# Linear attention and a bilinear GLU on one core: an order found offline, uneven row blocks, denominators on four partition groups, GpSimd out of layernorm, Wq turned by DMA

## The chip, the cores and the metric

The kernel runs on one core of one Trainium2 chip. The core has a matrix engine (TensorE, PE in the profile, with PEld for its weight loads), a vector engine (VectorE, DVE), an activation engine (ScalarE, ACT), a general engine (GpSimd, POOL) and an engine that here only issues transfers (SyncE, SP). Each runs its own program in order and waits on semaphores for the others. The metric is the device time of one execution in microseconds; smaller is better.

## What is computed

Two sublayers on x of 2048 rows by 640 columns, all inputs bf16: layernorm and linear attention of 32 heads of 20 columns with a learned feature map (a softmax of +pq and one of -pq, side by side), then layernorm and a gated unit without a nonlinearity.

```python
def A(x, wqkv, w_phi, wo):                       # 32 heads, Dh = 20
    q, k, v = heads(x @ wqkv)
    pq, pk = q @ w_phi, k @ w_phi                # per head, 20 x 20
    phi_q = concat(softmax(pq), softmax(-pq))    # 40 features
    phi_k = concat(softmax(pk), softmax(-pk))
    kv, z = phi_k.T @ v, sum_over_rows(phi_k)    # per head
    o = (phi_q @ kv) / (phi_q @ z + 1e-6)
    return o @ wo
def B(x, w_gate, w_up, w_down):                  # F = 1536
    return ((x @ w_gate) * (x @ w_up)) @ w_down
h = x + A(layernorm(x), ...)
out = h + B(layernorm(h), ...)
```

## The kernel before

**Tiles and stages.** Rows come in 16 tiles of 128. Attention cannot start on queries until kv and z are summed over all rows, so the kernel has a first part over all tiles and a second one in blocks.

The *first part*, tile by tile: load x, statistics of layernorm (`ln_stats`, L669 and L671 on DVE; `ln_rs`, L591 on ACT and L677 on DVE), the row apply (`ln_apply`: L682 if on ACT, L685 if on DVE, L687 if on POOL), a transposing DMA into `xnT` (L574, on SP). Then the V projection and the K projection, ten matmuls each (`proj`, recorded by `mm` at L580), two exponentials of K on ACT (L591), and `normalise`: a row sum (L721) and a reciprocal (L723) on DVE into a buffer of `sr`, of which there are four, and a multiplication by it on POOL (L597, `r<-r,sr`). `kv_acc` then adds the tile to three PSUM accumulators with eleven matmuls over groups of six heads. The feature weights `w_phi` are folded into Wk and Wq ahead: `fold_T` turns a weight chunk on PE (25 transposes at L698 and five copies at L608 or L609 per weight), `fold_M` multiplies it with a block-diagonal `Phi` (30 matmuls) and `copy` brings the result back to SBUF (L609, `wq<-ps`). Wk is folded at the start, Wq after tile 3.

The *second part* has four blocks of four tiles (512 rows). `q_proj` projects Q, takes four exponentials on ACT, a row sum (L757), a reciprocal (L759) and a multiplication on POOL (L597, `phq<-phq,sr`), and turns the tile by DMA into `pqT`. `num` computes, for six groups of heads, numerators and denominators in one matmul: `KV` (filled by `kv_evac`, L597 and L826) holds z in its first six columns, so the first six PSUM rows of a product are denominators. ACT takes Ln and Exp of these six rows by 512 columns (L591, `lnd` and `rden`), PE spreads the result over the heads' rows with the 0/1 matrix `Em`, ACT (L875) or DVE (L876) copies that out, and DVE multiplies (L597). `watt` applies Wo and adds the residual (L888), centres the row (L892 on ACT, L893 on DVE, L894 on POOL), turns it by DMA into `hT`, and squares it in place for the variance (L896). `fu` computes gate and up for one of 12 column chunks (ten matmuls of 512 columns), `fd` applies w_down and the residual (L926) and stores.

**What sets the order.** The functions do not issue instructions; they record them with their reads, writes, buffers and an estimated cost (`Recorder.add`, `R.group` for PE's groups). Where an operation could run on several engines, `alts` lists the others. `schedule` builds the dependence graph, replays the list on the estimated costs in `simulate` several times with changing priorities, and keeps the order and the choice of engines of the shortest replay. `resolve` then finds the waits, and `emit` writes every engine's program in that fixed order. Buffers of a pool, and PSUM banks, are handed out in that replay too: an instruction that needs a buffer waits on the chip for the one that used it last. Transfers stand on SP's queue in the same fixed order.

The profile shortens buffer names: `r` stands for `r1` (Wk and Wq work space, `phik`, later `w_down` and the GLU's products) and `r2` (V, later the attention's output, gate copies and output tiles).

Of the kernel before, what the change touches and what calls it, by code (L numbers as in the profile page):

```python
# [134 lines left out]
class Recorder:  # L135
# [125 lines left out]
    def simulate(self, key, back=False):  # L261
# [28 lines left out]
        def try_start(e):  # L290
            skipped, got = [], None
            while ready[e]:
# [11 lines left out]
                for b in sorted(u.bufs, key=lambda b: b.n):  # L304
# [59 lines left out]
    def schedule(self):  # L364
        self.graph()
        units = self.units
        best = None
# [9 lines left out]
        best = self.simulate(best_key)  # L377
# [108 lines left out]

def bass_sequential_preLN__linear_kernel_hedgehog__glu_gated_bilinear__prompt_kernel(
# [5 lines left out]
def _build(ctx, nc, A_x, A_wqkv, A_w_phi, A_wo, B_w_gate, B_w_up, B_w_down, out):  # L493
# [10 lines left out]
    hT = xnT_r[:, :].rearrange("p (b c n) -> p b c n", b=NB, c=NC)  # L504
# [30 lines left out]
    pqT_p = Pool("pqT", [sb("pqT", NCH * 512)[:, :], wkv_r[:, 0:NCH * 512]])  # L535
    xn_p = pool("xn", sb("xn", 3 * D), 0, D, 3)
    KV = view(sb("KV", NCH * P), "p (c n) -> p c n", c=NCH)
# [11 lines left out]
    Em = sb("Em", P)  # L549
# [20 lines left out]
    def dma(dst, src, nbytes, reads=None, writes=None, tr=False, eng="sync"):  # L570
        rd = [src] if reads is None else reads
        wr = [dst] if writes is None else writes
        if tr:
            return R.add("sync", lambda e: e.dma_start_transpose(real(dst), real(src)), rd, wr,  # L574
                         cost=0.4 + 0.55 * nbytes / 163840, lat=1.3, dma=1.25 * nbytes / 163840)
        return R.add(eng, lambda e: e.dma_start(real(dst), real(src)), rd, wr, cost=0.5, lat=1.5, dma=nbytes / 350e3)

    def mm(o, l, r, start, stop, skip=False):
        kw = {"skip_group_check": True} if skip else {}
        return R.add("tensor", lambda e: e.matmul(real(o), lhsT=real(l), rhs=real(r), start=start, stop=stop, **kw),  # L580
                     [l, r], [o], cost=max(0.06, numel(r) / 2400.0 + 0.0025), lat=0.17)

    def act(o, i, func, scale=1.0, bias=None):
# [8 lines left out]
        return R.add("scalar", go, rd, [o], cost=0.17 + n / 1200.0, lat=0.08)  # L592

    def tt(eng, o, a, b, op):
        n = numel(o)
        cost = 0.18 + 0.0017 * n if eng == "gpsimd" else (n + 130) / 960.0
# [54 lines left out]
    memset("gpsimd", vaug[:, :, :].rearrange("p t (h e) -> p t h e", e=E21)[:, :, :, DH:E21], 1.0)  # L651
    phq_clear = memset("gpsimd", phq_r[:, :].rearrange("p (k n) -> p k n", n=P)[:, :, 80:P], 1.0)
    memset("gpsimd", KV[:, 10, 0:HG], 0.0)
    memset("gpsimd", G6[:, :], 1.0)
    memset("gpsimd", Em[:, :], 1.0)
# [7 lines left out]
    afsel(Em[:, :], ALU.is_ge, 0.0, -HG, [[1, P]], -DH)  # L663
    afsel(Em[:, :], ALU.is_ge, 0.0, HG + DH - 1, [[-1, P]], DH)
# [15 lines left out]
    def ln_apply(t, dst):  # L680
# [3 lines left out]
              [x_all[:, t, :], mv[:, t, 0:5]], [k], cost=0.86, lat=0.08,  # L684
              alts=[("vector", lambda e: e.tensor_scalar(out=real(k), in0=x_all[:, t, :], scalar1=mv[:, t, 0:1],  # L685
                                                         scalar2=mv[:, t, 3:4], op0=ALU.subtract, op1=ALU.mult), 0.7),
                    ("gpsimd", lambda e: e.tensor_scalar(out=real(k), in0=x_all[:, t, :], scalar1=mv[:, t, 0:1],  # L687
                                                         scalar2=mv[:, t, 3:4], op0=ALU.subtract, op1=ALU.mult), 1.1)])
# [3 lines left out]
    def fold_T(w, a):  # L692
        pb = psum.new(1)
        tb = pb.bitcast(BF16)
        with R.group():
            for a2 in range(NC):
                o, i = tb[:, P * a2:P * (a2 + 1)], Wnat[w][:, a2, P * a:P * (a + 1)]
                R.add("tensor", lambda e, o=o, i=i: e.transpose(out=real(o), in_=i, identity=ident[:, :]),  # L698
                      [i, ident[:, :]], [o], cost=0.08, lat=0.17)
        copy("any", WT[w][:, a, :], tb[:, 0:D])  # L700

    def fold_M(w, i, dst):
        pr = psum.new(2)
        first = [True, True]
        with R.group():
            for a in range(NC):
                lo, hi = CH[a]
                for (h0, h1, half) in [(lo, min(hi, 24), 0), (max(lo, 25), hi, 1)]:
                    if h0 > h1:
# [4 lines left out]
                       first[half], False, skip=True)  # L714
# [102 lines left out]
    def kv_evac(c, n):  # L817
# [7 lines left out]
        o, i = KV[0:kr, c:c + n, 0:nh], psv[:, :, :, DH]  # L825
# [4 lines left out]
    pqT = {}  # L830
    num_u = {}

    def q_proj(t):
        b, tt_ = divmod(t, 4)
        if b not in pqT:
            pqT[b] = pqT_p.new()
        pr = psum.new(2)
        with R.group(hold=[pqT[b]]) as u:
            proj(pr, t, Wq)
        if b >= 1:  # L840
            R.after(mark["kv_proj"], u)
            R.after(mark["q0"], u)
        elif t == 0:
            mark["q0"] = u
            R.after(phq_clear, u)
        if b >= 2:
            R.after(num_u[b - 2], u)
        k = phq_p.new()
        soft_q(pr[:, 0:D], k)
        dma(pqT[b].rearrange("p (c n) -> p c n", c=NCH)[:, :, P * tt_:P * (tt_ + 1)], k, NCH * 32768, tr=True)  # L850
# [4 lines left out]
    def num(b, c):  # L855
        if c == 0:
            oT[b] = oT_p.new()
        h0, nh, kr = chunk_heads(c if c < NG else 10)
        m = HG + DH * nh
        pr = psum.new(2)  # L860
# [182 lines left out]
```

## Time and profile before

| | |
|---|---|
| time, median of 3 runs | 331.82 us (331.55 to 333.7) |
| the profiled execution | 334.79 us, of which the span from its first to its last instruction is 333.1 us |
| mean granted TensorE clock | 0.964 |
| busy over the span | PE 302.5 us (91%), DVE 171.7 (52%), ACT 158.1 (47%), POOL 117.1 (35%) |
| DMA | 55466 packets, 25.82 MB; HBM read 11.87 MB, written 2.62 MB |

All times in a profile are in us from the span's start unless marked ns. A timeline row has start, length, engine, line, operation, output<-input, count; in brackets the engine's idle time before it and what ended that wait. A row of the groups has engine, line, operation, shapes and count, then busy time and mean ns of one, then idle time before them. A mean clock below 1.00 in a stage means that the matrix engine ran part of it at half speed.

### The profile page before, as it was taken

How to read it: one execution, taken by the hardware profiler on the slowest of the kernel's cores; microseconds unless marked ns; L12 is line 12 of the kernel's file. 1: busy time of each engine (PE TensorE's matmuls, PEld its weight loads, DVE VectorE, ACT ScalarE, POOL GpSimd, SP SyncE). 2: the span in 40 equal slices, each digit the busy share in tenths (PEclk: the TensorE clock that was granted, in tenths of full speed). 3: DMA queues.
4: the chain of work that ended last, by engine and by line, in shares of the span. 5: the costliest groups of instructions: out<-in, count | busy, mean ns of one | idle time of the engine just before them, and what ended most of it. 6: DMA issues, size and time to landing. Idle time of an engine off the chain costs nothing.

```text
span 333.1 us, 4763 instructions
## 1 busy us (share of the span) xinstructions
PE 302.5 (91%) x1890; PEld 156.2 (47%) x1890; DVE 171.7 (52%) x288; ACT 158.1 (47%) x333; POOL 117.1 (35%) x74
## 2 busy tenths in 40 slices
PE   2899759699977888999999999999999999999996
PEld 2656525355652333544445434445544445544453
DVE  3896455786666388756332265623245542233332
ACT  4886547476627556847221373542065264022200
POOL 8899777799586044755000000500000000000000
PEclk9999899799977599999999999999999999999999
DMA  7667025486947205645202100321100030100011
GB/s 245 171 146 213 10 50 159 122 206 218 229 127 161 45 5 100 108 90 99 45 0 59 41 0 0 61 44 41 52 8 0 2 68 14 59 0 2 0 39 61
DMA packets 55466, 25.82 MB, mean 78 GB/s; under 512 B 45935, under 2 KB 54163, under 8 KB 55443
## 3 DMA queue, kind: packets, MB, share of 16 engines
q1 hardware_dynamic: 53299, 22.89, 28.5%
q10 hardware_dynamic: 2144, 2.62, 2.5%
q8 instruction: 15, 0.25, 0.3%
q14 instruction: 8, 0.07, 0.1%
HBM read 11.87 MB, written 2.62 MB: 44 GB/s over the span
## 4 chain that ended last, share of the span: by engine, by line
PE 69%; POOL 16%; DVE 8%; issue 3%; ACT 2%; DMA 2%; DVEq 0%
PE ps L580 68%; POOL r L597 7%; POOL xn L687 5%; POOL phq L597 4%; DVE sr L721 3%; DMA r<-in_A_wqkv_dram 2%; DVE sr L757 1%; DVE r L597 1%; DVE x_all L888 1%; PE ps L698 1%; DVE r L876 1%; POOL xn L894 1%; ACT r L591 0%; ACT r L609 0%; DVE xn L893 0%
## 5 line engine op out<-in xcount | busy, mean ns | idle before, releaser
L580 PE MATMUL ps<-xnT,wgu 128*128 128x512 bf16 x480 | 106.6, 379 | 0.4 <-DVE r L597 0.2
L591 ACT ACTIVATE r<-ps 128x640 bf16<-128x640 f32 (+1 forms) x96 | 60.3, 648 | 76.3 <-PE ps L580 75.4
L597 DVE TENSOR_TENSOR r<-ps,r 128x512 bf16<-128x512 f32 (+2 forms) x72 | 48.2, 686 | 54.1 <-PE ps L580 47.5
L580 PE MATMUL ps<-r 128*128 128x512 bf16 (+5 forms) x620 | 71.2, 274 | 5.4 <-POOL r L597 2.7
L580 PEld LDWEIGHTS ps<-xnT,wgu 128*128 128x128 bf16 x480 | 45.9, 98 | 57.3 <-issue 1.8
L580 PEld LDWEIGHTS ps<-r 128*128 128x128 bf16 (+2 forms) x620 | 45.8, 111 | 30.8 <-POOL r L597 3.1
L580 PE MATMUL ps<-wkv,xnT 128*128 128x512 bf16 x320 | 48.7, 311 | 8.0 <-ACT wq L609 3.8
L597 POOL TENSOR_TENSOR phq<-phq,sr 128x1320 bf16<-128x1320 bf16 x16 | 38.6, 2424 | 24.6 <-DVE sr L759 16.9
L580 PEld LDWEIGHTS ps<-wkv,xnT 128*128 128x128 bf16 x320 | 25.4, 101 | 28.5 <-ACT wq L609 4.2
L597 POOL TENSOR_TENSOR r<-r,sr 128x1280 bf16<-128x1280 bf16 x16 | 37.3, 2356 | 3.7 <-DVE sr L721 3.7
L721 DVE TENSOR_REDUCE sr<-r 128x64 f32<-128x1280 bf16 x16 | 23.6, 1477 | 21.6 <-POOL r L597 15.7
L926 DVE SCALAR_TENSOR_TENSOR r<-ps,mv,x_all 128x640 bf16<-128x640 f32 x16 | 14.1, 883 | 36.0 <-PE ps L580 36.0
L591 ACT ACTIVATE phq<-ps 128x600 bf16<-128x600 f32 (+1 forms) x64 | 23.7, 443 | 15.8 <-PE ps L580 15.7
L580 PE MATMUL ps<-wo,r 126*128 126x512 bf16 x192 | 30.0, 300 | 0.7 <-DVE x_all L888 0.6
L580 PE MATMUL ps<-wq,xnT 128*128 128x512 bf16 (+1 forms) x160 | 28.4, 335 | 1.1 <-DVE r L597 1.1
L894 POOL TENSOR_SCALAR xn<-x_all,mv 128x640 bf16<-128x640 bf16 x4 | 7.5, 1883 | 60.4 <-DVE mv L602 58.6
L757 DVE TENSOR_REDUCE sr<-phq 128x66 f32<-128x1320 bf16 x16 | 24.2, 1520 | 8.2 <-POOL phq L597 4.0
L687 POOL TENSOR_SCALAR xn<-x_all,mv 128x640 bf16<-128x640 bf16 x10 | 24.9, 2498 | 8.6 <-DVE mv L677 8.6
L580 PEld LDWEIGHTS ps<-wo,r 126*128 126x128 bf16 x192 | 13.9, 97 | 16.3 <-issue 5.5
L580 PEld LDWEIGHTS ps<-wq,xnT 128*128 128x128 bf16 x160 | 13.7, 108 | 14.4 <-issue 5.5
L876 DVE CAST r<-ps 126x512 bf16<-126x512 f32 (+1 forms) x14 | 9.5, 687 | 19.4 <-PE ps L580 19.4
L591 ACT ACTIVATE lnd<-ps 6x512 f32<-6x512 f32 (+1 forms) x24 | 13.4, 580 | 12.6 <-PE ps L580 12.6
(56 smaller groups left out, 184.1 us busy)
## 6 DMA issues: line engine op xcount, KB each, us to landing
out_dram<-r SPq DMA_DIRECT2D x16, 160.0 KB, 1.8
x_all<-in_A_x_dram ACTq DMA_DIRECT2D x3, 640.0 KB, 4.6
wgu<-in_B_w_gate_dram SPq DMA_DIRECT2D x5, 384.0 KB, 4.7
wgu<-in_B_w_up_dram SPq DMA_DIRECT2D x5, 384.0 KB, 4.0
r<-in_B_w_down_dram SPq DMA_DIRECT2D x6, 320.0 KB, 4.6
r<-in_A_wqkv_dram SPq DMA_DIRECT2D x2, 800.0 KB, 5.1
wkv<-in_A_wqkv_dram SPq DMA_DIRECT2D x1, 800.0 KB, 10.0
wo<-in_A_wo_dram SPq DMA_DIRECT2D x4, 157.5 KB
```

Source lines behind the costliest of these rows:

```text
L580: return R.add("tensor", lambda e: e.matmul(real(o), lhsT=real(l), rhs=real(r), start=start, stop=stop, **kw), [l, r], [o], cost=max(0.06, ...
L591: return e.activation(out=real(o), in_=real(i), func=func, scale=scale, **kw)
L597: return R.add(eng, lambda e: e.tensor_tensor(out=real(o), in0=real(a), in1=real(b), op=op), [a, b], [o], cost=cost)
L687: ("gpsimd", lambda e: e.tensor_scalar(out=real(k), in0=x_all[:, t, :], scalar1=mv[:, t, 0:1], scalar2=mv[:, t, 3:4], op0=ALU.subtract, op ...
L698: R.add("tensor", lambda e, o=o, i=i: e.transpose(out=real(o), in_=i, identity=ident[:, :]), [i, ident[:, :]], [o], cost=0.08, lat=0.17)
L721: R.add("vector", lambda e: e.tensor_reduce(out=real(sr)[:, 0:n], in_=real(v), axis=AX.X, op=ALU.add), [v], [sr[:, 0:n]], cost=0.13 + n * ...
L757: R.add("vector", lambda e: e.tensor_reduce(out=real(r4(0)), in_=real(k4), axis=AX.X, op=ALU.add), [k4], [r4(0)], cost=0.13 + n * DH / 960.0)
L876: alts=[("vector", lambda e: e.tensor_copy(real(o), real(i)), 0.67)])
L888: R.add("vector", lambda e: e.scalar_tensor_tensor(out=h, in0=real(pr)[:, 0:D], scalar=1.0, in1=h, op0=ALU.mult, op1=ALU.add, accum_out=sm ...
L894: ("gpsimd", lambda e: e.tensor_scalar(out=real(k), in0=h, scalar1=nm, scalar2=None, op0=ALU.add), 1.1)])
L926: R.add("vector", lambda e: e.scalar_tensor_tensor(out=real(k), in0=real(pr)[:, 0:D], scalar=r2, in1=h, op0=ALU.mult, op1=ALU.add), [pr[:, ...
```

## The change

Six things are changed together.

1. **The order** is no longer searched while the program is built: a table `ORDER` of 1088 priorities, found offline, is replayed once. Some cost estimates are changed with it, and buffers are taken in the order of pool names. Every engine's program is reordered by this.
2. **Row blocks** are 2, 2, 4, 4 and 4 tiles (`BLK`) in place of 4, 4, 4 and 4. The first two blocks' numerators, gate and up matmuls have 256 columns. `q_proj` of the first two tiles no longer waits for all K and V projections by an explicit edge, and the edges between blocks are gone.
3. **Denominators of the first two blocks** (`num_first`): z is kept in a matrix `Zd` of 32 columns per group of heads. Up to four groups write their denominators to rows 0, 32, 64 and 96 of one PSUM bank, so that one Ln and one Exp over 128 rows by 256 columns serve four groups, and a second pair over 64 rows the other two. `Em` becomes four matrices, one for each starting row. The other blocks do it as before, with z copied from `Zd` into `KV`.
4. **GpSimd** has no row applies any more, neither in the first layernorm nor in the second; two memsets go from it to DVE, and memsets of the larger `Em` and of `Zd` come to it.
5. **Wq** is turned by five transposing DMAs straight out of DRAM, in place of one plain load, 25 transposes on PE and five copies.
6. **The square** of the second layernorm reads the row itself with the mean as bias and writes to `junk`, where it squared the centred row in place after its DMA.

```diff
-        best = self.simulate(best_key)
+        if len(ORDER) == len(units):
+            return {u: float(k) for u, k in zip(units, ORDER)}
...
+        best = self.simulate(self.keys())
...
+ORDER = [int(k) for k in """
+6 0 16 7 1 11 12 24 2 17 19 13 30 43 49 39 45 51 5 8 3 14 27 10 4 15 18 9 29 32 21 25 22 34 37 42 56 58 61 66 69 73 47 52 36 40 44 48 38 46 50 53 20
...
-    hT = xnT_r[:, :].rearrange("p (b c n) -> p b c n", b=NB, c=NC)
+    BLK = ((0, 2), (2, 2), (4, 4), (8, 4), (12, 4))
+    hT = [xnT_r[:, t * D:(t + n) * D].rearrange("p (c n) -> p c n", c=NC) for t, n in BLK]
...
-    memset("gpsimd", vaug[:, :, :].rearrange("p t (h e) -> p t h e", e=E21)[:, :, :, DH:E21], 1.0)
-    phq_clear = memset("gpsimd", phq_r[:, :].rearrange("p (k n) -> p k n", n=P)[:, :, 80:P], 1.0)
+    memset("vector", vaug[:, :, :].rearrange("p t (h e) -> p t h e", e=E21)[:, :, :, DH:E21], 1.0)
+    phq_clear = [memset("vector", phq_r[:, :].rearrange("p (c n) -> p c n", n=P)[:, :, 120:P], 1.0),
...
+    memset("gpsimd", Zd[:, :, :], 1.0)
...
               alts=[("vector", lambda e: e.tensor_scalar(out=real(k), in0=x_all[:, t, :], scalar1=mv[:, t, 0:1],
-                                                         scalar2=mv[:, t, 3:4], op0=ALU.subtract, op1=ALU.mult), 0.7),
-                    ("gpsimd", lambda e: e.tensor_scalar(out=real(k), in0=x_all[:, t, :], scalar1=mv[:, t, 0:1],
-                                                         scalar2=mv[:, t, 3:4], op0=ALU.subtract, op1=ALU.mult), 1.1)])
+                                                         scalar2=mv[:, t, 3:4], op0=ALU.subtract, op1=ALU.mult), 0.7)])
...
-        o, i = KV[0:kr, c:c + n, 0:nh], psv[:, :, :, DH]
+        o, i = Zd[0:kr, c:c + n, 0:nh], psv[:, :, :, DH]
...
+    def num_first(b):
+        oT[b] = oT_p.new()
+        q, n = pqT[b], P * BLK[b][1]
+        den = psum.new(1)
+        lnd, rden = lnd_p.new(), rden_p.new()
+        for k, cs in enumerate(((0, 1, 2, 3), (4, 5))):
+            bank = den[:, n * k:n * (k + 1)]
+            with R.group() as u:
+                for s in range(2):
+                    for j, c in enumerate(cs):
+                        kr = 120 if c < NG else 80
+                        ck = (NG * s + c) if c < NG else 10
+                        if c < NG or s == 0:
+                            mm(bank[32 * j:32 * j + 32, :], Zd[0:kr, ck, :], q[0:kr, ck, :], s == 0, s == 1 or c == NG,
+                               cost=0.06 if j else 0.25)
+            R.after(mark["kv_acc"], u)
+            w = 32 * len(cs)
+            act(lnd[0:w, n * k:n * (k + 1)], bank[0:w, :], ACT.Ln)
+            act(rden[0:w, n * k:n * (k + 1)], lnd[0:w, n * k:n * (k + 1)], ACT.Exp, scale=-1.0)
+        for c in range(6):
+            pr = psum.new(2)
+            nh, m, n = num_mm(b, c, pr)
+            r0, k = 32 * (c % 4), c // 4
+            expand(b, c, pr, m, Em[r0:r0 + nh, c % 4, 0:m], rden[r0:r0 + nh, n * k:n * (k + 1)])
...
-        R.add("scalar", lambda e: e.activation(out=real(k), in_=real(k), func=ACT.Square, accum_out=ss), [k], [k, ss],
-              cost=0.9, lat=0.08)
+        R.add("scalar", lambda e: e.activation(out=junk[:, :], in_=h, func=ACT.Square, bias=nm, accum_out=ss), [h, nm],
+              [junk[:, :], ss], cost=0.95, lat=0.08)
...
-            R.after(tr_u[5], load_w(Wnat[1], 0))
-            for a in range(NC):
-                fold_T(1, a)
+            for k in range(NC):
+                u = dma(WT[1][:, :, P * k:P * (k + 1)], A_wqkv[P * k:P * (k + 1), 0:D], 163840, reads=[], tr=True)
+                R.after(tr_u[5], u)
...
+    copy("any", KV[:, :, 0:HG], Zd[:, :, 0:HG])
```

Three places of the new order follow. A row of the order has line, operation, output<-input, the output's shape and how often it stands there in a row; the line numbers of the changed kernel are its own.

POOL in the first part, before: row applies (`xn`) stand between the normalisations of K (`r<-r,sr`).

```order
L687 TENSOR_SCALAR xn<-x_all,mv 128x640 x5
L597 TENSOR_TENSOR r<-r,sr 128x1280 x5
L687 TENSOR_SCALAR xn<-x_all,mv 128x640 x2
L597 TENSOR_TENSOR r<-r,sr 128x1280
L687 TENSOR_SCALAR xn<-x_all,mv 128x640
L597 TENSOR_TENSOR r<-r,sr 128x1280
```

POOL there now, from the making of `Phi` on to the end of its program:

```order
L645 TENSOR_TENSOR r<-Wrows,Gm 128x160
L645 TENSOR_TENSOR r<-Wrows,Gm 128x140 x4
L645 TENSOR_TENSOR r<-r,sr 128x1280 x8
L645 TENSOR_TENSOR phq<-phq,sr 128x11x120
L645 TENSOR_TENSOR r<-r,sr 128x1280 x3
L645 TENSOR_TENSOR phq<-phq,sr 128x11x120
L645 TENSOR_TENSOR r<-r,sr 128x1280 x5
L645 TENSOR_TENSOR phq<-phq,sr 128x11x120 x14
```

The ten row applies are gone, and two tiles of Q, where it was four, are normalised ahead of the last of K.

SP's queue from its start, before: the third row of `in_A_wqkv_dram` is Wq's plain load, behind seven turns of x tiles.

```order
L576 DMA r<-in_A_wqkv_dram 128x5x640
L576 DMA Wrows<-in_A_w_phi_dram 128x5x20
L576 DMA wkv<-in_A_wqkv_dram 128x5x640
L574 DMA_TRANSPOSE xnT<-xn 128x5x128 x7
L576 DMA r<-in_A_wqkv_dram 128x5x640
L574 DMA_TRANSPOSE xnT<-xn 128x5x128 x5
```

SP's queue from its start now:

```order
L624 DMA r<-in_A_wqkv_dram 128x5x640
L624 DMA Wrows<-in_A_w_phi_dram 128x5x20
L624 DMA wkv<-in_A_wqkv_dram 128x5x640
L622 DMA_TRANSPOSE xnT<-xn 128x5x128 x6
L622 DMA_TRANSPOSE r<-in_A_wqkv_dram 128x5x128
L622 DMA_TRANSPOSE xnT<-xn 128x5x128 x2
L622 DMA_TRANSPOSE r<-in_A_wqkv_dram 128x5x128 x4
```

Five transposing DMAs out of DRAM stand where the load stood, the first behind six turns of x tiles, the other four behind eight; the rows of `Wo` and of the gate and up weights come after them, and the ninth turn of x behind those.

ACT behind the last accumulation, before: Ln and Exp of six rows for each group of heads (`lnd`, `rden`), and the copies of the expanded denominators (L875).

```order
L591 ACTIVATE lnd<-ps 6x512 x2
L591 ACTIVATE rden<-lnd 6x512 x2
L591 ACTIVATE lnd<-ps 6x512
L875 ACTIVATE r<-ps 126x512
L591 ACTIVATE rden<-lnd 6x512
L875 ACTIVATE r<-ps 126x512
L591 ACTIVATE lnd<-ps 6x512 x2
```

ACT at the same place now, with a Q tile's exponentials (`phq<-ps`) between:

```order
L639 ACTIVATE lnd<-ps 128x256
L639 ACTIVATE phq<-ps 128x2x20
L639 ACTIVATE rden<-lnd 128x256
L657 ACTIVATE KV<-Zd 128x11x6
L913 ACTIVATE r<-ps 126x256
L639 ACTIVATE phq<-ps 128x5x120
L639 ACTIVATE lnd<-ps 64x256
L639 ACTIVATE phq<-ps 128x40
L913 ACTIVATE r<-ps 126x256
```

One Ln and one Exp over 128 rows now serve four groups of heads; the copy of the sums into `KV`, for the numerators' first six columns, stands behind them.

More of the change, by code (lines that the diff above doesn't have):

```diff
@@ L879, in watt @@
     def watt(t):
[L880 removed]
+        b = block_of(t)
+        n, q = P * BLK[b][1], P * (t - BLK[b][0])
         pr = psum.new(2)
```

169 lines of the change are left out of this document (90 added, 79 removed), and 29 rows, old and new, of the table ORDER.

## The prediction

> **What bounds the kernel now.** I read the split of the chain of waits by engine first, then the busy times cut into four stages, then the timeline where TensorE (PE) stands still. The split says that PE carries 69% of the chain and GpSimd (POOL) 16%:
>
> ```profile
> PE 69%; POOL 16%; DVE 8%; issue 3%; ACT 2%; DMA 2%; DVEq 0%
> ```
>
> Where POOL's share lies is told by the stages: from the first V projection to the end of the K^T V accumulation, from there to the first gate/up matmul, and from there to the last matmul, with the tail. Columns: length; busy time and count of PE, weight loads, DVE, ACT, POOL; granted clock; DMA share and GB/s.
>
> ```profile
> 13.01:99.60 86.59, 73.52 (x632) 46.00 (x632) 59.13 (x94) 53.46 (x105) 72.83 (x32) 0.94 0.56 146
> 99.60:144.58 44.98, 38.82 (x191) 16.69 (x190) 31.59 (x57) 30.72 (x72) 20.08 (x10) 0.85 0.45 86
> 144.58:329.90 185.32, 184.28 (x1018) 88.03 (x1016) 73.13 (x118) 65.89 (x142) 12.62 (x6) 1.00 0.14 33
> 329.90:333.10 3.20, 0.00 (x0) 0.00 (x0) 0.88 (x1) 0.00 (x0) 0.00 (x0) 0.94 0.14 51
> ```
>
> In the third stage PE is busy 184.3 of 185.3 us at full clock: nothing there is to be had but work. In the first two it is busy 112 of 131.6 us, part of that at half clock: 0.94 is 12% of 86.6 us at half, 0.85 is 30% of 45 us, together 24 us. POOL is the fullest engine beside PE in the first, 72.8 of 86.6 us. How it stops PE is seen at one knot of the timeline:
>
> ```profile
> 42.47 2.36 POOL L597 TENSOR_TENSOR r<-r,sr 128x1280 bf16<-128x1280 bf16 x1
> 44.86 1.49 DVE L721 TENSOR_REDUCE sr<-r 128x64 f32<-128x1280 bf16 x1 [5.64 <-POOL r L597]
> 46.45 0.92 ACT L682 ACTIVATE xn<-x_all,mv 128x640 bf16<-128x640 bf16 x1 [5.79 <-DVE mv L677]
> 47.28 0.68 ACT L609 ACTIVATE wq<-ps 128x640 bf16<-128x640 f32 x1
> 48.02 2.31 PE L580 MATMUL ps<-wkv,xnT 128*128 128x512 bf16 x15 [3.83 <-ACT wq L609]
> ```
>
> POOL's normalisation frees one of the four sr buffers; DVE's row sum waited 5.64 us for it, the layernorm factor stands behind that sum, ACT's layernorm behind the factor, the copy that frees a PSUM bank behind that, and PE 3.83 us behind the copy. POOL was late because layernorm rows stood between its normalisations.
>
> **The sum: work without waits.** PE's prices, from rows with no wait (start to start):
>
> ```profile
> 80.10 4.24 PE L580 MATMUL ps<-wkv,xnT 128*128 128x512 bf16 x30
> 84.17 2.88 PE L580 MATMUL ps<-wq,xnT 128*128 128x512 bf16 x20
> 86.89 2.82 PE L580 MATMUL ps<-r 128*120 128x126 bf16 x47
> ...
> 139.07 5.58 PE L580 MATMUL ps<-wo,r 126*128 126x512 bf16 x36
> ...
> 196.92 0.42 PE L580 MATMUL ps<-rden,Em 6*126 6x512 bf16 x1
> 197.28 2.33 PE L580 MATMUL ps<-xnT,wgu 128*128 128x512 bf16 x10
> ...
> 289.67 26.06 PE L580 MATMUL ps<-xnT,wgu 128*128 128x512 bf16 x120
> 315.57 14.29 PE L580 MATMUL ps<-r 128*128 128x512 bf16 x104
> ```
>
> A projection (ten matmuls) is 4.07/3 = 1.36 us, an accumulation matmul 2.82/47 = 0.06, an output-projection tile 5.58/3 = 1.86, a gate/up matmul 25.9/120 = 0.216 and a numerator matmul with as many columns the same, a denominator expansion 0.36, of which 0.145 is more than its 512 columns take (the change to 6 rows). A matmul of 256 columns I put at half and 0.003 more, 0.11.
>
> Before, between 13.0 and 144.6 us, PE does 32 V and K and 15 Q projections (63.9), 176 accumulations (10.6), Wq's turning and folding (25 transposes, 30 products, at 0.06: 3.3), 22 numerator matmuls (4.7), 12 expansions (4.3), 7 output tiles (13.0): 99.8 us. The 131.6 us thus hold 32 us of waits and half clock, which is all that the change can win. After it, up to the same point, the order has 11 Q projections (43 in all, 58.5), the accumulations (10.6), 30 folding products (1.8), 22 numerators of 256 columns (2.4), 12 expansions (0.25 each, 3.0), the new 22 denominator matmuls (2.4) with eight changes between array shapes at 0.145 (1.2), 4 output tiles (7.4): 87.3 us. What has moved behind that point is 4 Q projections (5.4), 3 output tiles (5.6) and one block's numerators and expansions (11 x 0.216 + 6 x 0.36 = 4.5); 240 gate/up matmuls of 256 columns for 120 of 512 add 0.5. So the third stage is 185.3 + 16.0 = 201.3. With 13.0 ahead and 3.2 behind: 13.0 + 87.3 + 201.3 + 3.2 = 304.8 us if PE never waits.
>
> **The waits that stay**, part by part, from the costliest groups, one shape each (busy time, mean ns):
>
> ```profile
> L597 POOL TENSOR_TENSOR r<-r,sr 128x1280 bf16<-128x1280 bf16 x16 | 37.3, 2356 | 3.7 <-DVE sr L721 3.7
> L687 POOL TENSOR_SCALAR xn<-x_all,mv 128x640 bf16<-128x640 bf16 x10 | 24.9, 2498 | 8.6 <-DVE mv L677 8.6
> L721 DVE TENSOR_REDUCE sr<-r 128x64 f32<-128x1280 bf16 x16 | 23.6, 1477 | 21.6 <-POOL r L597 15.7 <-POOL phq L597 4.3 <-ACT r L591 1.4
> L669 DVE BATCH_NORM_STATS2 st<-x_all 128x6 f32<-128x320 bf16 x32 | 13.8, 474 | 3.8 <-DMA x_all<-in_A_x_dram 3.6
> L591 ACT ACTIVATE rden<-lnd 6x512 bf16<-6x512 f32 x20 | 11.7, 615 | 0.1
> L591 ACT ACTIVATE lnd<-ps 6x512 f32<-6x512 f32 x20 | 11.2, 580 | 11.8 <-PE ps L580 11.8
> L723 DVE RECIPROCAL sr<-sr 128x64 f32<-128x64 f32 x16 | 8.8, 547 | 0.3
> ```
>
> GpSimd out of layernorm: 24.9 us leave POOL, which up to the last accumulation then has 37.3 and two Q tiles, some 43 us from about 20 us on; it could be done at 63 and no longer binds. DVE takes seven of the ten row applies, four of them behind its first row sum, and has, from its first row sum near 17.3 us: 16 sums 23.6, 16 reciprocals 8.8, five Q tiles at a sum and a reciprocal each 10.1, 16 statistics 7.6, small ones and applies about 5 (estimate; DVE was busy 59.1 us there before): 55.1, so it could be through at 72.4. PE's own work to that point (32 projections, 5 Q, folds, accumulations, 62.7 us) ends at 75.7. ACT gains three applies, loses four fold copies, and had 53.5 us in 86.6. DVE is but 3 us ahead of PE and needs PE's results: I take 3 us of mutual waits, between 0 and 10.
>
> Wq turned by DMA: 25 transposes and five copies go; five transposing DMAs out of DRAM come, on SP's queue between the x transposes, so tiles 6 to 10 of x stand behind them. No such DMA is in the trace. The nearest rows:
>
> ```profile
> 64.54 2.53 SPq L574 DMA_TRANSPOSE xnT<-xn  x2
> ...
> xnT<-xn SPq DMA_TRANSPOSE x32, 2.6
> x_all<-in_A_x_dram ACTq DMA_DIRECT2D x2, 160.0 KB, 4.0
> wkv<-in_A_wqkv_dram SPq DMA_DIRECT2D x1, 800.0 KB, 10.0
> ```
>
> Issuing takes 1.27 us each, landing 2.6 (SBUF source) to 4.0 (160 KB out of DRAM). The five and two x tiles, begun near 25 us, are out at 34 and landed at 36.5 to 38; folding of the fourth piece is due near 33, and 2 to 5 us of wait follow if nothing reorders, part of it time that DVE needs anyway. I take 2, from 0; the other end is five such DMAs at 10.0 us each, one after another, last landing at 75, a wait of about 40.
>
> Uneven blocks and denominators: the chain behind the last accumulation now needs two Q tiles, not four, and four pairs of Ln and Exp on up to 128 rows by 256 columns (about 0.8 a pair, half of 1.195 and a fixed part) where 12 pairs of 1.195 us stood. It still begins with DVE's turn of K^T V out of PSUM,
>
> ```profile
> 95.11 0.66 DVE L597 TENSOR_TENSOR KV<-ps,G 120x480 bf16<-120x480 f32 x1 [0.92 <-PE ps L580]
> ```
>
> two such rows and eight small ones, some 2.4 us by estimate, then a Ln, an Exp and ACT's copy of the sums into KV, against one Q projection on PE: 2 us of wait. From there to the first gate/up matmul PE has 24.6 us, DVE about 23, ACT about 20: again 2 us, up to 6. [...] Memsets moved to DVE (before x lands), the unused Square wait, the buffers picked by pool name: no cost, since DVE and ACT are idle there; without that cover they'd be under 2 us.
>
> Sum: 304.8 + 3 + 2 + 2 + 2 + 1.5 = 315.3 us of span. The profiled execution took 334.79 for a span of 333.1, and stands 2.97 above the median 331.82: the median to expect is 315.3 + 1.7 - 3.0 = 314.0, **314 us**.
>
> **Rivals.** DVE becomes the bound. In two places DVE scaled a row while POOL was at work:
>
> ```profile
> 18.48 4.98 POOL L687 TENSOR_SCALAR xn<-x_all,mv 128x640 bf16<-128x640 bf16 x2
> 21.43 0.58 DVE L685 TENSOR_SCALAR xn<-x_all,mv 128x640 bf16<-128x640 bf16 x1
> ...
> 128.72 2.42 POOL L597 TENSOR_TENSOR phq<-phq,sr 128x1320 bf16<-128x1320 bf16 x1 [2.86 <-DVE sr L759]
> 129.98 1.35 DVE L893 TENSOR_SCALAR xn<-x_all,mv 128x640 bf16<-128x640 bf16 x1
> ```
>
> The first took 0.58 us inside a POOL row, the second 1.35 us and ended 0.19 behind the POOL row's end, as if held. If each of the four applies is held for a normalisation of 2.36, DVE is through at 82, and starved in between nearer 85; nine us on PE's end and the half clock that follows give 322. [...]
>
> The order's waits are covered (PE dense): 304.8 + 2 to 3, about 306; against it speaks that before even the best stretch ahead of 99.6 us had waits. Slower than before: Wq's pieces come so late that PE waits over 28 us more than without waits (304.8 + 28 = 332.8, where the span was 333.1). That takes about 7.5 us a piece; at 10.0 it gives 304.8 + 40 = 345, and all the rest of x behind them. No 160 KB row comes near. The order does not do what it says: it was found on costs, not on the chip, and the 32 us of waits come back elsewhere, 330.
>
> **How the numbers follow.** Waits of 4 to 16 us, the forecast: 0.60, 307 to 320. Covered: 0.12, 303 to 307. DVE bound: 0.20, 318 to 326. Wq late: 0.05. No gain: 0.03. The range 303 to 325 takes in the bound without waits and most of the DVE case. Faster by over 1% (below 328.5; 1% is about what a measurement here tells from no change) 0.92, within 1% 0.03, slower 0.05.
>
> **What would show it.** First gate/up matmul at 108 to 114 us (before 144.58); the last accumulation at 80 to 84; POOL idle a third of the time up to there; PE's busy share behind the first gate/up matmul still 99% over some 201 us; at most two spells at half clock. Wrong if transposing DMAs out of DRAM land later than 5 us, if DVE applies show means above 1.3 us, or if PE waits in the third stage for the output tiles of four-tile blocks, whose transposes now have some 5 us of other work to hide behind.

## The result, and the profile after

| | time, us (median, lowest to highest, runs) | ratio to before, 95% interval |
|---|---|---|
| before | 332.1 (331.55 to 333.7, 4) | |
| changed kernel | 311.78 (309.66 to 316.35, 4) | 0.936 [0.930, 0.942] |
| changed kernel, timed again | 310.9 (308.25 to 312.86, 6) | 0.935 [0.931, 0.939] |

The change takes 6.4% off the time. Ratios here and below are of the executions within 1.5% of the fastest of their kernel, which leaves the one of 316.35 us out of the first. The profiled execution is that one, with a span of 314.6 us. TensorE's mean granted clock was 0.978 in it and 1.000 in the shortest: 2.2% of the span is 6.9 us, which is the whole distance to 309.66. So most of the scatter of these four is time at half clock; in the six of the repeat it is only a part (below). In the two spells of the profiled execution the granted clock is 0.50, and the ten matmuls of a projection that lie in the first take 2.87 us, where they take 1.52 at 1.00.

The split of the chain of waits by engine:

```profile
PE 77%; DMA 9%; POOL 6%; DVE 4%; ACT 1%; SPq 1%; issue 0%
```

POOL's 16% has become 6%, and DMA, at 2% before, is second. The stages of the changed kernel, cut at the same events as before (first V projection, last accumulation, first gate/up matmul, last matmul) with the same columns:

```profile
0.00:12.32 12.32, 5.38 (x55) 4.41 (x56) 7.60 (x24) 7.58 (x14) 6.47 (x26) 1.00 0.85 257
12.32:82.70 70.38, 65.58 (x590) 41.58 (x594) 55.74 (x96) 49.92 (x97) 45.91 (x20) 0.98 0.75 169
82.70:110.41 27.71, 26.49 (x157) 12.27 (x155) 18.08 (x40) 16.20 (x48) 11.13 (x6) 0.82 0.57 100
110.41:311.40 200.99, 200.99 (x1231) 107.07 (x1229) 95.86 (x163) 84.49 (x188) 19.04 (x8) 1.00 0.19 38
311.40:314.60 3.20, 0.00 (x0) 0.00 (x0) 0.88 (x1) 0.00 (x0) 0.00 (x0) 1.00 0.29 102
```

The first part is 16.2 us shorter (70.38 for 86.59), the second 17.3 (27.71 for 44.98), the third 15.7 longer (200.99 for 185.32), since work has moved behind the first gate/up matmul. In the first two PE stands still for 6.0 us in all, where it was 19.2 before. The three kinds of wait behind it, of PE from 13 to 110 us (in total, times, longest):

```profile
PE ps L628 <- DMA r<-in_A_wqkv_dram: 3.4, 1, 3.4
PE ps L628 <- DMA xnT<-xn: 1.4, 3, 0.6
PE ps L628 <- ACT lnd L639: 1.2, 1, 1.2
```

POOL is not among them. But the chain of waits still runs through it up to the end of the first part:

```profile
60.56 2.40 POOL r L645
62.96 2.38 POOL phq L645
65.34 2.33 POOL r L645
...
69.72 9.30 POOL r L645 x4
79.03 2.45 POOL phq L645 x2
81.47 5.63 DMA pqT<-phq
...
88.11 23.89 PE ps L628 x135
```

POOL's normalisations end when PE's accumulations need them, and the transpose of a Q tile follows. ACT waits 1.93 us for that transpose, since it frees a buffer of `phq`, and the Ln that PE needs (`lnd`) stands behind it in ACT's order; so PE's wait of 1.22 us is the end of this chain. For the rest PE had other work at hand. An engine can be on the chain and cost little.

### The profile page after: what moved, and what is told of

Its sections match the earlier page's. It is cut to its first block, busy times and chain, and to the rows that moved or that the text cites. A ratio compares the mean times of both kernels' runs of the same rounds, so it can differ in the third digit from the quotient of the medians.

```text
span 314.6 us, 5099 instructions
## 1 busy us (share of the span) xinstructions
PE 298.4 (95%) x2024; PEld 165.3 (53%) x2024; DVE 178.2 (57%) x321; ACT 158.2 (50%) x345; POOL 82.5 (26%) x58
## 4 chain that ended last, share of the span: by engine, by line
PE 77%; DMA 9%; POOL 6%; DVE 4%; ACT 1%; SPq 1%; issue 0%
PE ps L628 77%; POOL r L645 4%; DMA r<-in_A_wqkv_dram 4%; DMA xnT<-xn 3%; DVE sr L768 2%; DMA pqT<-phq 2%; POOL phq L645 2%; PE ps L745 1%; SPq L622 1%; DVE sr L770 1%; ACT phq L639 0%; DVE st L718 0%; DVE xn L734 0%; DVE r L1003 0%; DVE wkv L656 0%
## 5 line engine op out<-in xcount | busy, mean ns | idle before, releaser
L628 PE MATMUL ps<-xnT,wgu 128*128 128x512 bf16 (+1 forms) x600 | 106.6, 337 | 0.0
L639 ACT ACTIVATE r<-ps 128x640 bf16<-128x640 f32 (+2 forms) x108 | 62.8, 595 | 73.8 <-PE ps L628 73.1
L645 DVE TENSOR_TENSOR r<-ps,r 128x512 bf16<-128x512 f32 (+5 forms) x90 | 51.5, 581 | 63.2 <-PE ps L628 51.8
L628 PEld LDWEIGHTS ps<-xnT,wgu 128*128 128x128 bf16 x600 | 57.8, 98 | 46.3 <-issue 1.7
L628 PE MATMUL ps<-r 128*128 128x512 bf16 (+5 forms) x620 | 72.8, 269 | 3.8 <-DMA r<-in_A_wqkv_dram 3.4
L628 PEld LDWEIGHTS ps<-r 128*128 128x128 bf16 (+2 forms) x620 | 44.0, 108 | 31.3 <-DMA r<-in_A_wqkv_dram 3.6
L628 PE MATMUL ps<-wq,xnT 128*128 128x512 bf16 (+1 forms) x160 | 25.3, 309 | 1.2 <-ACT lnd L639 1.2
L964 DVE SCALAR_TENSOR_TENSOR x_all<-ps,x_all 128x640 bf16<-128x640 f32 x16 | 13.2, 823 | 11.7 <-PE ps L628 11.5
L639 ACT ACTIVATE lnd<-ps 6x512 f32<-6x512 f32 (+3 forms) x22 | 11.9, 547 | 11.6 <-PE ps L628 11.3
L914 DVE CAST r<-ps 126x512 bf16<-126x512 f32 (+2 forms) x14 | 8.6, 615 | 15.4 <-PE ps L628 15.3
L968 ACT ACTIVATE xn<-x_all,mv 128x640 bf16<-128x640 bf16 x9 | 7.4, 827 | 17.3 <-DVE mv L650 17.3
```

Source lines behind the costliest of these rows:

```text
L639: return e.activation(out=real(o), in_=real(i), func=func, scale=scale, **kw)
L645: return R.add(eng, lambda e: e.tensor_tensor(out=real(o), in0=real(a), in1=real(b), op=op), [a, b], [o], cost=cost)
L914: lat=0.08, alts=[("vector", lambda e: e.tensor_copy(real(o), real(i)), (n + 130) / 960)])
L964: R.add("vector", lambda e: e.scalar_tensor_tensor(out=h, in0=real(pr)[:, 0:D], scalar=1.0, in1=h, op0=ALU.mult, op1=ALU.add, accum_out=sm ...
L968: R.add("scalar", lambda e: e.activation(out=real(k), in_=h, func=ACT.Identity, bias=nm), [h, nm], [k], cost=0.83, lat=0.08, alts=[("vecto ...
```

## Experiments

All ratios are to the kernel before, run beside it on the same chip. `control`, `wq_early`, `pool_ln` and `no_table` ran on one chip and the others on a second, so across the two groups the ratios are what to compare.

### The same kernel again

`control` has no edit.

> The changed kernel itself, once more. Both theories: 309 to 313 us in most runs. If spells at half clock make the spread between its runs (the profiled execution had two spells, 13.7 us together, and 316.35 us; an execution with a mean clock of 1.000 took 309.66), then span and mean clock of each run go together: about 1.7 us for each spell of 3.4 us.

0.935 [0.931, 0.939]. Its profiled execution (312.61 us, clock 0.989) has the wait for Wq again (3.8 us) and the others at 0.5 or less, and one spell at half clock (35.5 to 42.4 us) where the first trace had two. Its second stage:

```profile
83.50:106.70 23.20, 22.08 (x153) 11.00 (x156) 17.90 (x40) 16.10 (x48) 11.55 (x6) 1.00 0.63 116
```

The same instructions took 23.2 us at full clock and 27.7 at 0.82. That difference between two traces of one kernel is larger than any wait left in it.

That time and clock go together came only in part. Two executions at a clock of 1.000 took 308.25 and 310.31 us, and one at 0.995 took 312.86: some 3 us of scatter are left that the clock does not account for.

### The order taken away

`no_table` keeps the rest of the change and lets the build search the order, as before:

```diff
-ORDER = [int(k) for k in """
...
-""".split()]
+ORDER = []
```

> The table emptied, so that the order is searched at build as before; blocks, denominators, GpSimd, Wq and the square stay as changed. Theory (the parts of the change carry the gain, the table a smaller share): 314 to 322. Rival (the table carries it): 327 to 333, near the kernel before.

0.976 [0.974, 0.979], median 324.41 us; one of its four runs took 1056 us. The number lies between the theory's and the rival's: without the list two thirds of the gain are gone. The first two stages:

```profile
12.80:81.10 68.30, 61.87 (x556) 39.74 (x566) 54.22 (x85) 48.51 (x92) 43.55 (x19) 0.98 0.70 159
81.10:117.60 36.50, 29.16 (x172) 14.18 (x173) 22.29 (x47) 18.04 (x53) 12.92 (x6) 0.81 0.41 91
```

The first part is as short as with the list. The loss is behind the last accumulation, 36.5 us for 23.2 to 27.7: PE idle for 7.3 us, and at a clock of 0.81.

### GpSimd given back, and taken away alone

`pool_ln` is the changed kernel, list included, with GpSimd again allowed for row applies:

```diff
+                    ("gpsimd", lambda e: e.tensor_scalar(out=real(k), in0=x_all[:, t, :], scalar1=mv[:, t, 0:1],
+                                                         scalar2=mv[:, t, 3:4], op0=ALU.subtract, op1=ALU.mult), 1.1)])
...
```

> The table and all else kept, but GpSimd may take row applies of layernorm again where the replay gives them to it (seven in the first part, against ten before the change). Theory (the gain of the first part comes from GpSimd having nothing but normalisations): its late normalisations hold back the end of the accumulation by 3 to 10 us, time 315 to 322. Rival (the order found offline is what counts): within 2 us of the control.

0.978 [0.976, 0.981], 324.73 us: 13.8 us above the repeated changed kernel, more than the theory had. POOL took seven of the applies. Its group (busy time, mean ns of one):

```profile
L736 POOL TENSOR_SCALAR xn<-x_all,mv 128x640 bf16<-128x640 bf16 x7 | 17.8, 2550 | 6.1 <-DVE mv L726 5.9
```

The code prices such an apply at 1.1 us; it takes 2.55. A planner that can't see 1.45 us of each hands GpSimd work that is late. What PE then waits for, up to 118 us, is turned tiles of x above all (0.5 us in the repeat):

```profile
PE ps L628 <- DMA xnT<-xn: 6.5, 4, 2.5
```

The list was found for a kernel without these alternatives, and part of the loss may be that.

`before_no_pool_ln` strikes the same two alternatives from the kernel before and changes nothing else.

> The kernel before with one edit: GpSimd is struck from the engines that may apply a layernorm; the order is searched at build. Theory (GpSimd's row applies held back the first part): the last accumulation comes at 80 to 86 us instead of 97.8, the time falls to 318 to 325. Rival (without the table the gain is lost in the first part too): 329 to 333.

0.990 [0.987, 0.994], 329.59 us, some 3 us, the rival's number. Here my theory failed: it had POOL's applies as what stopped PE before, and with them gone only 1% is won. The first two parts did shrink, by 9.7 and 5.7 us, but 10.0 of that come back in the third, into which work has moved:

```profile
13.10:90.00 76.90, 67.81 (x621) 43.91 (x631) 63.84 (x99) 56.83 (x110) 51.02 (x22) 1.00 0.64 154
90.00:129.30 39.30, 32.54 (x131) 13.31 (x132) 25.42 (x47) 26.10 (x59) 12.82 (x6) 0.74 0.53 105
129.30:324.60 195.30, 192.31 (x1053) 92.45 (x1072) 82.23 (x132) 70.64 (x156) 12.07 (x5) 0.99 0.14 33
```

POOL fell from 72.8 to 51.0 us in the first part, and PE still idles 9.1, 6.8 and 3.0 us in the three, 18.8 in all, where it was 20.3 before. The three largest of its waits from 13 to 130 us (in total, times, longest):

```profile
PE ps L580 <- DVE r L597: 4.2, 4, 1.7
PE ps L580 <- POOL r L597: 2.9, 2, 1.6
PE ps L580 <- ACT phq L591: 2.7, 1, 2.7
```

No one engine owns them, and the clock of 0.74 in the second part gives back what the first, now at 1.00, had won.

### The order alone, and with GpSimd out

For these the kernel before got a list of its own: random moves of one or a few priorities for ten minutes, kept when the kernel's own replay on its own cost estimates got shorter. The list is read as in the change:

```diff
+        if len(ORDER) == len(units):
+            best_key = {u: float(k) for u, k in zip(units, ORDER)}
         best = self.simulate(best_key)
...
```

`order_alone` has every instruction of before; `order_no_pool_ln` is without GpSimd in layernorm and has a list found for that.

> The kernel before, every instruction of it, with a list of priorities of its own, found by ten minutes of random moves that were kept when the planner's costs made the program shorter (GpSimd may still take row applies: 7 in the first part, and some of the second layernorm's). Theory (order and GpSimd's applies are each worth about 13 us, as the list taken away and the applies given back each cost 13.5 and 13.8 us): the order gains what it can while GpSimd is still in, 316 to 324 us. Rival 1 (the order is worth something only with the uneven blocks and the turned Wq, since it is their small pieces that it places): 328 to 332. Rival 2 (the order is nearly all of the change): 309 to 314.

0.988 [0.983, 0.993], 329.04 us.

> The kernel before with GpSimd out of layernorm and a list of its own, found in the same way; blocks of four, denominators by group and Wq turned on TensorE stay. Theory (list and GpSimd out carry the gain together; blocks and turned Wq are worth a few us once each version has its own list): 312 to 318 us, and 5 to 10 us below the run with the order alone. Rival 1 (the blocks and the turned Wq carry 12 us, as the version with even blocks and no list cost): 321 to 326. Rival 2 (with a list, GpSimd in layernorm costs nothing): within 2 us of the run with the order alone.

0.955 [0.950, 0.960], 317.79 us, in the theory's range.

So the order alone is worth 1.2%, GpSimd out alone 1.0%, and both together 4.5%, twice their sum. That one list came out better than the other in the search is not the reason: the kernels' own replay puts the two at 299.1 and 299.8 us, while the chip has them 11 us apart. For the order alone the first rival's number came, but not for its reason: with GpSimd out the order pays without any uneven block. What stops the order alone is seen in its chain of waits, ahead of the last accumulation and again ahead of the first gate/up matmul:

```profile
72.94 2.70 DVE sr L767 x2
...
75.70 13.94 POOL r L643 x6
...
89.69 1.72 PE ps L626 x14
...
123.18 5.61 POOL xn L940 x3
128.79 4.78 POOL phq L643 x2
```

Six normalisations stand back to back on POOL, behind the seven applies of some 2.5 us that the replay had put at 1.1, and PE waits 5.5 us in all for such normalisations; later three applies of the second layernorm (`xn`) hold a Q tile in the same way. The first two parts of the order alone, and then those of the order with GpSimd out, with POOL busy for 67.3 of 81.3 us and for 50.1 of 78.0:

```profile
13.90:95.20 81.30, 71.55 (x621) 45.75 (x631) 62.45 (x100) 53.33 (x105) 67.33 (x29) 0.98 0.68 163
95.20:143.30 48.10, 41.12 (x209) 17.76 (x211) 32.98 (x60) 30.96 (x73) 24.03 (x11) 0.86 0.42 78
```

```profile
14.10:92.10 78.00, 68.94 (x620) 44.18 (x631) 64.07 (x100) 55.98 (x111) 50.09 (x22) 0.98 0.69 160
92.10:131.20 39.10, 35.59 (x187) 15.83 (x189) 32.07 (x58) 30.20 (x72) 16.74 (x8) 0.91 0.48 89
```

The first part differs by 3.3 us and the second by 9.0, of which 2.6 come back in the third. In the second part PE idles 7.0 us for 3.5, and its clock is 0.86 for 0.91. By the replay the prices account for about half: with 2.5 and 1.88 us, as measured, for POOL's two kinds of apply, the replay of the order alone, each instruction on the engine it had, is 305.1 us in place of 299.1. A list found with right prices and GpSimd still allowed was not run.

### Blocks, denominators and Wq

`even_blocks` has no list, four blocks of four and denominators by group; GpSimd stays out and Wq is turned by DMA. It is to be read against `no_table`.

```diff
-    BLK = ((0, 2), (2, 2), (4, 4), (8, 4), (12, 4))
+    BLK = ((0, 4), (4, 4), (8, 4), (12, 4))
...
-    num_first(0)
+    num(0)
...
```

> The changed kernel without the table, and with four blocks of four tiles, denominators per group of heads, as before; to be set beside the run without the table (324.4). Theory (two-tile blocks shorten the way from the last accumulation to the first gate/up matmul): that way is 42 us or more instead of 36.7, less 12 to 16 us of work that is then done ahead, net slower by 2 to 6: 326 to 331. Rival (block sizes bring nothing without the right order): 323 to 326.

1.012 [1.008, 1.017], 336.8 us, slower than before, beyond both the theory's and the rival's range, and 12.4 us above `no_table` (3.6% by the ratios). The loss is not only behind the last accumulation, 46.4 us for 36.5: the first part is longer too, 76.6 for 68.3, and 5.1 come back in the third. From `before_no_pool_ln` (0.990) it differs in Wq's DMAs, the place of z and the small edits, cost estimates among them. In an order that is searched at the build these cost 2% rather than save; which of them does was not told apart.

`den_by_group` and `wq_on_pe` keep the change's priorities for all that is unchanged, and put the new pieces where the old ones stood.

```diff
-    num_first(0)
+    num(0)
...
-    num_first(1)
+    num(1)
...
```

> The table's priorities kept, but the first two blocks take denominators per group of heads from the numerators' first six rows: twelve pairs of Ln and Exp of 6 rows by 256 columns instead of four pairs, no denominator matmuls. Theory (ACT is nearly full between the last accumulation and the first gate/up matmul): 16 more ACT rows of 0.4 us, 6.4 us, of which half or more is felt: 314 to 318. Rival (covered): 309 to 312. The clock: if small matmuls on few rows or columns let the clock fall, its spells near 88 us should change too.

0.957 [0.951, 0.962], 318.22 us, 7.3 above the repeated changed kernel, at the end of the theory's range. But what PE waits for up to 118 us is mostly DVE's products, 4.1 us in six waits, and ACT's rows for 1.7, so ACT's extra rows are not shown to be the way it is lost.

```diff
-            for k in range(NC):
-                u = dma(WT[1][:, :, P * k:P * (k + 1)], A_wqkv[P * k:P * (k + 1), 0:D], 163840, reads=[], tr=True)
-                R.after(tr_u[5], u)
...
+            R.after(tr_u[5], load_w(Wnat[1], 0))
+            for a in range(NC):
+                fold_T(1, a)
```

> The table's priorities kept, Wq loaded plainly and turned on PE as before (25 transposes, five copies placed just ahead of the folds). Theory (the DMA turns cost PE a wait of 3.4 to 3.8 us and save it 1.4 us and two engines five copies): within 1% of the control's 310.9. Rival (the copies hold back ACT and DVE, which are nearly full): 314 to 320.

0.971 [0.967, 0.975], 323.23 us, 12.3 above, past the rival's range as well. Either Wq on PE is dear, or a list made for other pieces no longer fits. `wq_on_pe_own` is the same kernel with a list searched for it.

> The changed kernel with Wq turned on TensorE again, as in the earlier run of that part (323.2 us), but with a list found for it instead of the changed kernel's own list with the new pieces put in. Theory (the 12 us of the earlier run were mostly a list that no longer fitted; the 25 transposes are 3 to 4 us of TensorE): 312 to 316 us. Rival (the turned Wq is really worth 12 us, by TensorE's, ScalarE's and VectorE's time in the first part): 320 to 325.

0.977 [0.969, 0.984], 326.69 us: no better, though the replay has this list at 298.5 us, 1.6 longer than the change's own. The loss is in the first part, 81.0 us for 70.8 in the repeat. Yet `order_no_pool_ln` turns Wq on PE as well and takes 317.79. So it isn't the 25 transposes by themselves, some 1.5 us of PE at the 0.06 us each that the prediction took (in the trace of the kernel before, 20 of them take 1.29 us); in these lists Wq on PE costs with two short blocks ahead and not with four even ones. Why is not settled. In its chain the normalisations of K carry the end of the first part:

```profile
73.04 6.99 POOL r L699 x3
80.03 2.38 POOL phq L699
82.42 6.95 POOL r L699 x3
89.37 2.39 POOL phq L699
91.78 5.95 DMA pqT<-phq
```

### Wq's pieces earlier, and another list

`wq_early` issues two of Wq's five DMAs ahead of the turns of x tiles 6 and 7, and changes nothing else:

```diff
...
+            for a in pieces[1:3]:
+                self.ops.remove(a)
+                self.ops.insert(self.ops.index(first), a)
...
```

> Two of the four late pieces of Wq are issued ahead of the turns of x tiles 6 and 7; nothing else moves. Theory (the pieces' landing is a wait on PE's path): the wait of 3.4 us before the fold falls below 1 us, the half clock spell behind it goes, the time falls by 3 to 5 us to 306 to 309. Rival (the wait only moves to the projections of tiles 6 and 7, or DVE needs the time anyway): 310 to 312, as the control.

0.933 [0.931, 0.936], 309.39 us. The 3.4 us wait for Wq is gone from its trace, and so are the spells at half clock in that execution. Against the repeated changed kernel's 0.935 [0.931, 0.939] the gain can't be told from none. PE's waits up to 110 us are 4.4 us in all in its trace and 5.6 in the repeat's, so most of that wait has gone elsewhere, as the rival had it.

`own_table` is the changed kernel with another list, found from its own by the same random moves with Wq's landing put at 5 us:

```diff
...
+                u.ops[0].lat = 5.0
                 R.after(tr_u[5], u)
```

> The changed kernel with another list, found by the same random moves from the changed kernel's own list, with the landing of Wq's five transposing DMAs put at 5 us in the planner (1 us there before), so that it issues them earlier; every instruction is the same. Theory (the list's worth is that of any list from such a search, and Wq's wait of about 3 us goes): 307 to 311 us, 1 to 3 us below the changed kernel. Rival 1 (the changed kernel's list has something that such a search doesn't give): 313 to 320. Rival 2 (no difference that can be told): 310 to 312.

0.942 [0.937, 0.948], median 316.49 us (313.46 to 346.31; the longest of the six had a clock of 0.85). The first rival's number came. The wait for Wq is gone, and PE waits 5.8 us in all for turns of x, a Q tile's turn and a normalisation of K. At a clock of 0.993 it took 313.46 us; the changed kernel at 0.994 and 0.995 took 311.49 and 312.86. The replay has my list 3.8 us shorter with that landing (296.5 for 300.3), the chip has it no shorter: at some us the kernel's replay no longer ranks lists.

No version here is shown to beat the changed kernel.

## Why the prediction was right, and where not

**The total.** 314 was forecast, 311.78 came, in the range and near the middle of the likeliest case. The sum for the profiled span was 315.3; it is 314.6. The median is lower by more than that because I took the profiled execution to stand 3.0 us above it, as it did before; here it stands 4.6 above, with the clock of 0.978.

**The marks.** Last accumulation forecast at 80 to 84 us: 82.7, and 83.5 in the repeat. First gate/up matmul at 108 to 114: 110.4, and 106.7. Third stage 201.3 us, 99% busy: 201.0, without a wait (201.0 in the repeat). POOL idle a third of the time to the last accumulation: 45.9 us busy of 70.4, 35% idle. At most two spells at half clock: two.

**The terms, and some luck.** 87.3 us of work were priced up to the first gate/up matmul. From the stage rows, less what half clock takes (half of PE's busy time in the spells): 65.58 - 1.7 and 26.49 - 4.9 give 85.5; the repeat, whose spell cost 2.7 (5.4 of its 6.8 us were busy), 65.72 - 2.7 + 22.08 = 85.1. The pricing was some 2 us too high. The waits were put at 9 us and came to 6.0: 1.4 for turned tiles of x where 3 us of mutual waits were forecast, 3.4 for Wq where it was 2, and 1.2 behind the last accumulation where it was 4. The time ahead of the first V projection was 12.3 for 13.0. Against these stands the last term of the sum, 1.5 us for half clock, which no run shows: in its place the two spells of this trace last 3.4 and 10.2 us and cost 6.6, the one of the repeat lasts 6.8 and costs 2.7, and the trace of `wq_early` has none. So terms that were 1.8, 3.0 and 0.7 us too high, with 0.3 in the third stage, and one that was 5.1 too low nearly cancel; that the sum is right to 0.7 us is partly luck.

**Wq.** Forecast: 2 us of wait, and wrong "if transposing DMAs out of DRAM land later than 5 us". Two of the five did; the wait is 3.4 us. The issues on SP's queue and the landing of the group (median):

```profile
25.37 1.28 SPq L622 DMA_TRANSPOSE xnT<-xn  x1
26.69 5.24 SPq L622 DMA_TRANSPOSE r<-in_A_wqkv_dram  x4
```

```profile
x_all<-in_A_x_dram ACTq DMA_DIRECT2D x3, 640.0 KB, 6.5
...
r<-in_A_wqkv_dram SPq DMA_TRANSPOSE x5, 4.3
```

Issuing took 1.3 us each as priced. The piece that PE waited for landed 7.1 us behind its issue, beside a 640 KB load of x begun at the same time. The rival "Wq late" (7.5 us for every piece) was not far off in its price for one piece, but PE waited for one piece only.

**POOL, the step that failed.** The prediction named POOL's row applies as what made PE wait before and let "could be done at 63" follow from taking them out. POOL was not done at 63 but at 81.5, on the chain: it idled 35% of the time for inputs that came late, and then had four normalisations of K and two of Q back to back from 69.7 on. And taking the applies out alone won 1.0%, not the larger part of 6.4. What the runs show in its place: the 32 us of waits and half clock have no one owner. Without the applies, an order that is searched while the program is built leaves PE waiting for DVE, POOL's normalisations, ACT and DMA, 18.8 us for 20.3. With the applies, another order gains 9 us in the replay (299.1 for 308.3) and 3 to 4 on the chip. Only the pair pays, 4.5%. That it loses by POOL's applies, priced at less than half, is what its chain and the replay at measured prices say, for about half of the difference; the other half is open. My sum was right, beside the luck above, because it priced the state with both, and the working of PE without waits didn't need to know whose waits they were. Attributing them to one knot of the timeline did, and one knot is one instance.

The other 2%, blocks, denominators and Wq together, holds for the change's list. With lists of my own it is less: 0.942 (`own_table`, whose search began at the change's list) against 0.955 (`order_no_pool_ln`). How it divides among the three stays open, since each one's removal under a kept list also spoils the list.

**DVE as the bound, the rival at 0.20.** It did not happen: DVE's applies in the first part took 413 ns in the mean, against my bound of 1.3 us. But single applies came near that bound and above it. The two groups (busy, mean ns):

```profile
L734 DVE TENSOR_SCALAR xn<-x_all,mv 128x640 bf16<-128x640 bf16 x8 | 3.3, 413 | 0.7 <-DMA xnT<-xn 0.7
L969 DVE TENSOR_SCALAR xn<-x_all,mv 128x640 bf16<-128x640 bf16 x7 | 5.1, 726 | 0.1
```

None of the eight began inside a POOL row. Of the seven behind them three did, and here are two:

```profile
112.99 2.42 POOL L645 TENSOR_TENSOR phq<-phq,sr 128x1320 bf16<-128x1320 bf16 x1 [0.51 <-DVE sr L806]
114.31 1.29 DVE L969 TENSOR_SCALAR xn<-x_all,mv 128x640 bf16<-128x640 bf16 x1
```

```profile
158.04 2.43 POOL L645 TENSOR_TENSOR phq<-phq,sr 128x1320 bf16<-128x1320 bf16 x1 [1.90 <-DVE mv L650]
158.90 1.75 DVE L969 TENSOR_SCALAR xn<-x_all,mv 128x640 bf16<-128x640 bf16 x1
```

The first ends at 115.60, 0.19 behind POOL's end at 115.41, the second at 160.65, 0.18 behind 160.47; the third, of 0.50 us from 103.23, ends 0.19 behind as well. The four that began outside a POOL row take 0.39. But the apply of 0.58 us that the prediction shows from the kernel before also began inside a POOL row, and ended 1.45 us ahead of that row's end. So what holds an apply is not shown. The rival put each of its four at 2.36 us; the longest here took 1.75, and the change's list lets none of the eight begin inside a POOL row. The three that do are off PE's path (PE has no wait from 88.1 us on), and cost nothing here.

## What to carry to other kernels

Two causes of one wait can each look worthless when removed alone; try the pair before dropping either. A planner's list is worth what its prices are worth: measure the operation that a slow engine takes (1.1 us assumed, 2.5 measured) before searching on it, and don't judge a part by taking it out under a list that was tuned with it in. When waits are down to a few us, the time at half clock is the next term (a cost of 6.6 us in one trace of the changed kernel, of 2.7 in the other), and it differs from run to run, so compare several runs, with their clocks beside them.

## What was not expected of the hardware

**The clock fell while PE was busy.** The second spell at half clock began at 87.6 us. In the 3.4 us ahead of it PE was busy for 2.7, with small matmuls:

```profile
84.46 0.32 PE L628 MATMUL ps<-rden,Em 6*126 6x256 bf16 x1
84.71 0.39 PE L628 MATMUL ps<-pqT,Zd 120*32 120x256 bf16 x3
85.03 0.43 PE L628 MATMUL ps<-pqT,KV 120*126 120x256 bf16 x2
85.39 0.32 PE L628 MATMUL ps<-rden,Em 6*126 6x256 bf16 x1
...
86.52 0.38 PE L628 MATMUL ps<-wq,xnT 128*128 128x512 bf16 x1
88.11 2.42 PE L628 MATMUL ps<-wq,xnT 128*128 128x128 bf16 x9 [1.22 <-ACT lnd L639]
```

Of the one wait there, 1.22 us, 0.75 lie ahead of the fall. The first spell began at 36.4, when PE had waited 3.4 us for Wq; in the repeat the clock fell at 35.5, when PE had waited 2.7 of its 3.84 us. The second is a fall with far less waiting ahead of it. The spell then lasted to 97.9, with PE busy for 9.8 of its 10.2 us.

What decides is not shown. In the trace of the kernel before, PE waited 3.83 us up to 48.02, and the granted clock was 1.00 from 42.6 to 63.0. Of the 2.66 us that PE was busy ahead of 87.6, expansions (`rden`, 6 rows) are 0.95 and denominator matmuls (`Zd`, 32 columns) 0.39, but no run tried the small matmuls by themselves: `den_by_group`, which has no denominator matmuls, shows a mean clock of 0.5 and 0.7 in the slices from 86.9 to 102.7 us, as the changed kernel does there. In the repeat the same matmuls ran with a wait of 0.52 us in place of the 1.22, and no spell came.

**The spell is not the program's alone.** The first four runs of the changed kernel had mean clocks of 1.000, 0.994, 0.994 and 0.978 and took 309.66, 311.75, 311.82 and 316.35 us: what the clock is short of 1, times the span, is their scatter to within half a us. In the six of the repeat 3 us are left, from 308.3 to 311.3.
